# Out weights of the second layer made one group earlier and kept in DRAM, and the weights' place split in two regions

## The chip, the cores and the metric

The kernel runs on one core of a Trainium2 chip. The metric is the device time of one launch in microseconds (us). The kernel before has a median of 670.33 us over three runs (668.5 to 673.26).

## The reference, cut to what matters

The output of a banded attention with block summaries, 1536 tokens of width 512, goes through two feed-forward layers:

```python
def _moe_ref(x, w_gate, w_val, w_out, rms_g):        # first part: 512 -> 1536 -> 512
    xn = x / np.sqrt(np.mean(x * x, axis=-1, keepdims=True) + 1e-06) * rms_g
    g = xn @ w_gate
    return ((g / (1.0 + np.exp(-g))) * (xn @ w_val) @ w_out).astype(np.float32)

def _moe2_ref(x, w_in, w_out):                       # second part: 512 -> 2048 -> 512
    h = x @ w_in
    return ((h - np.tanh(h)) @ w_out).astype(np.float32)
```

The weights arrive as 64-bit floats. Each float32 operand of a product is split into a high and a low part, and three matmuls are summed.

## The kernel before, in words

**Stages.** The tokens are 12 tiles of 128, in three groups of four. Attention for a tile is two units of four heads. The first part (`step`, kind "a") runs over the groups; for each group it runs 12 steps, one for each block of 128 hidden columns: eight first products (three matmuls each, 128x512) into two "mid" banks, the gate on ACT and DVE, then four second products into four accumulator banks. While a group is in the first part, the attention units of the next group are woven in; the third group has none beside it. The second part (`pair`) runs over the groups again, eight pairs of hidden blocks each, by Strassen's scheme: seven products of 128x256 from sums of input and weight blocks, a tanh, and eight second products with the out weights of the pair's two blocks.

**Weights.** `widen` turns 512 columns of 64-bit weights into float32: a 512 KB load into one of two `raw` buffers, one ACT instruction (L737), two DVE instructions (L738, L739). `split` makes the high part by an ACT cast (L754, into `ih` or `oh`) and the low part by a subtraction on DVE or POOL (L756, into `il` or `ol`). There are three `oh` and three `ol` buffers. The first layer's 12 blocks of 1536 columns lie in one region `wd`; the second layer's 16 blocks of 1024 columns (512 in, 512 out) are widened into the same place as the first layer's blocks are finished with. So 32 conversions of 512 columns belong to the second layer.

**Second part, by group.** In its first group `make` forms the weight sums of a pair (L1028 to L1031), splits them (L1048, L1050), splits the two out blocks, and stores all of it in DRAM (`keep_i`, `keep_o`). In its second and third group `fetch` loads them: four transfers of `ki` and four of `ko` for each pair. The fetched sums land in `wd`, as nine buffers for the high and nine for the low parts (`lh`, `ll`), which can be used only once all of `wd` is done with; the second group's first pair lands in `ih` and `il` instead. The chain inside a pair is: products 1 and 6, a copy and an add (L1102, L1098), products 7 and 5, adds, products 4, 2 and 3.

**Order.** A planner (`Plan`) places every instruction on its engine by due time, with a duration and a lag for each, and the kernel is emitted in that order. Each engine then works its row strictly in order, SP too, which issues every transfer and waits there for its buffers. The planner counts a transfer at 2.78 us per MB (1.46 us for one `raw` load).

Of the kernel before, what the change touches and what calls it, by code (L numbers as in the profile page):

```python
# [9 lines left out]
F32 = mybir.dt.float32  # L10
# [246 lines left out]
def kernel(  # L257
# [24 lines left out]
    wd_r = Region(const, "wd", NF1 * W1, F32)  # L282
    wd = wd_r.get(F32)

    ident = const.tile([P, P], F32, name="ident")

# [88 lines left out]
                return tl[i][:, :, (t - t0) * P:(t - t0 + 1) * P]  # L375


    far = 4 * W1
    kr, vr = [], []
    for b in range(B):  # L380
        kr.append(wd[:, far:far + 4 * S])
        vr.append(wd[:, far + 4 * S:far + 8 * S])
        far += 8 * S
    early_u = [wd[:, 8 * W1 + i * UN:8 * W1 + (i + 1) * UN] for i in range(EARLY)]
    far = 8 * W1 + EARLY * UN
    early_s = [wd[:, far + i * HH * SC:far + (i + 1) * HH * SC] for i in range((4 * W1 - EARLY * UN) // (HH * SC))]
# [322 lines left out]


    def w_first(f):
        return wd[:, f * W1:(f + 1) * W1]

    def w_second(f):
        return wd[:, f * W2:(f + 1) * W2]

    chain = {}

# [178 lines left out]
    spare = NF2 * W2  # L897
    plan.pools["sm"] = Buffers([wd[:, spare:spare + 4 * q]])
    plan.pools["up"] = Buffers([rest.part(2 * 512, 2 * 512 + q, F32), const.tile([P, q], F32, name="up")])
    for i, tag in enumerate(("eh", "el")):  # L900
        plan.pools[tag] = Buffers([hi_r[k].part(i * 1024, (i + 1) * 1024, F32R) for k in range(2)])
    for i, tag in enumerate(("lh", "ll")):
        plan.pools[tag] = Buffers([wd_r.part(k * 1024, (k + 1) * 1024, F32R) for k in range(i, 18, 2)])
    plan.pools["tb"] = Buffers([lo_r[0].part(i * 512, (i + 1) * 512, F32) for i in range(NC_)])
    operand = {}
    ready = {}
    prepared = {}
# [68 lines left out]
    def dma_both(n, pick, slots, kept, *after):  # L976
# [10 lines left out]
            ops.append(o)  # L987
        return ops

    def fetch(n, g):  # L990
        weights = {}
        at = 0
        last_made = [chain[k] for k in ("i", "il", "o", "ol")]
# [7 lines left out]
        outs = []  # L1001
        for j in (1, 0):
            w = [slot("oh"), slot("ol")]
            o = dma_both(DM, True, w, keep_o[n][j], *stored[n])
            outs.insert(0, (*w, [o]))
        return outs, weights

    def make(n):
        f0, f1 = 2 * n, 2 * n + 1
        d = [w_second(f) for f in (f0, f1)]  # L1010
        conv = [wide_op["b", f][0] for f in (f0, f1)]
        a11, a12 = d[0][:, 0:q], d[0][:, q:2 * q]
        a21, a22 = d[1][:, 0:q], d[1][:, q:2 * q]
        right = wd[:, f0 * W2:(f0 + 2) * W2].rearrange("p (f c) -> p f c", f=2)[:, :, q:2 * q]
        weights = {}
        store = []

        if n:
            gate = [o for f in range(NF1 - 2, NF1) for o in split_op["a", f]] + first_ops["a", 2][-2:]
            names = "ih", "il", "sm"  # L1020
        else:
            gate = first_ops["a", 0] + first_ops["a", 1] + unit_ops
# [12 lines left out]
        for ks, pieces in zip(  # L1035
            turns,
            (
                ((0, q, lambda: a11, lambda t: t, [conv[0]]), (q, 3 * q, lambda: sm[:, 0:3 * q], lambda t: t, [o3])),
                ((0, 2 * q, lambda: right, three, conv), (2 * q, q, lambda: s(4), lambda t: t, [o4])),
            ),  # L1040
        ):
            wh, wl = slot(names[0]), slot(names[1])
            done = []
            for c, m, src, form, of in pieces:
                cut = slice(c, c + m)
                us = 0.1 + 0.42 * m / 512
# [15 lines left out]
        return outs, weights  # L1062

    def pair(g, n, at):
        f0, f1 = 2 * n, 2 * n + 1
# [20 lines left out]
            second_first.setdefault(g, []).append(o)  # L1086
            return o

        after_a = [o for f in range(NF1 - 2, NF1) for o in split_op["a", f]]
# [107 lines left out]
    for g in range(len(GROUPS)):  # L1197
# [8 lines left out]
        if g + 2 == len(GROUPS):  # L1206
            pass
    for f in range(NF2):
        over = [o for q in range(NF1) if q * W1 < (f + 1) * W2 and f * W2 < (q + 1) * W1 for o in split_op["a", q]]
# [116 lines left out]
```

## Time and profile before

| | |
|---|---|
| runs, median (lowest to highest) | 670.33 us (668.5 to 673.26) |
| profiled execution | 668.83 us, of it 666.9 us from the first to the last instruction |
| PE busy | 654.6 us (98%) |
| PE weight load busy | 553.9 us (83%) |
| DVE / ACT / POOL busy | 449.3 / 334.0 / 53.5 us |
| TensorE clock granted | 0.996, the higher of its two levels (2.4 GHz) |
| moved by DMA | 128.11 MB |

The stages lie about so in the profiled execution: attention alone up to 37 us; first part with attention 37 to 148 (first group) and 148 to 291 (second group); first part alone 291 to 397 (third group); second part 397 to 483, 483 to 567 and 567 to 652, then the last outputs.

### The profile page before, as it was taken

How to read it: one execution, taken by the hardware profiler on the slowest of the kernel's cores; microseconds unless marked ns; L12 is line 12 of the kernel's file. 1: busy time of each engine (PE TensorE's matmuls, PEld its weight loads, DVE VectorE, ACT ScalarE, POOL GpSimd, SP SyncE). 2: the span in 40 equal slices, each digit the busy share in tenths (PEclk: the TensorE clock that was granted, in tenths of full speed). 3: DMA queues.
4: the chain of work that ended last, by engine and by line, in shares of the span. 5: the costliest groups of instructions: out<-in, count | busy, mean ns of one | idle time of the engine just before them, and what ended most of it. 6: DMA issues, size and time to landing. Idle time of an engine off the chain costs nothing.

```text
span 666.9 us, 10381 instructions
## 1 busy us (share of the span) xinstructions
PE 654.6 (98%) x3714; PEld 553.9 (83%) x3714; DVE 449.3 (67%) x1007; ACT 334.0 (50%) x688; POOL 53.5 (8%) x118
## 2 busy tenths in 40 slices
PE   8999999999999999999999999999999999999996
PEld 7998777888888888788888888888888888888885
DVE  5789996885636355479877779898874443545343
ACT  3895566774636445457555548555542231323222
POOL 2221212110101100000000010101100000000000
PEclk9999999999999999999999999999999999999999
DMA  9887564662011110022745558668689999997232
GB/s 342 331 282 266 187 190 140 201 195 88 2 31 32 49 41 1 1 64 63 238 153 163 150 168 311 248 259 316 239 322 349 350 338 368 344 322 254 95 95 95
DMA packets 47642, 128.11 MB, mean 192 GB/s; under 512 B 5688, under 2 KB 8168, under 8 KB 47592
## 3 DMA queue, kind: packets, MB, share of 16 engines
q1 hardware_dynamic: 47592, 127.46, 55.6%
q8 instruction: 29, 0.48, 0.3%
q14 instruction: 21, 0.17, 0.1%
HBM read 101.23 MB, written 26.21 MB: 191 GB/s over the span
## 4 chain that ended last, share of the span: by engine, by line
PE 83%; DMA 8%; ACT 4%; DVE 3%; issue 1%; SPq 1%; POOL 0%; ACTq 0%; DVEq 0%; POOLq 0%
PE bank L779 14%; PE bank L781 13%; PE bank L780 13%; PE mid L779 12%; PE mid L780 11%; PE mid L781 11%; DMA raw<-in_w_dram 4%; PE bank L643 3%; PE bank L549 2%; PE bank L600 1%; DMA wd<-in_units_dram 1%; PE bank L654 1%; DMA out_dram<-th 1%; ACT wd L737 1%; DMA ko<-ol 1%
## 5 line engine op out<-in xcount | busy, mean ns | idle before, releaser
L779 PE MATMUL mid<-hi,ih 128*128 128x512 f32 (+1 forms) x310 | 123.5, 398 | 0.1
L781 PE MATMUL mid<-hi,il 128*128 128x512 f32 (+1 forms) x310 | 118.1, 381 | 0.0
L780 PE MATMUL mid<-lo,ih 128*128 128x512 f32 (+1 forms) x304 | 116.5, 383 | 0.0
L781 PE MATMUL bank<-oh,hl 128*128 128x512 f32 x192 | 75.7, 394 | 0.5 <-DVE hl L1136 0.5
L779 PE MATMUL bank<-oh,hh 128*128 128x512 f32 x192 | 75.8, 395 | 0.1
L780 PE MATMUL bank<-ol,hh 128*128 128x512 f32 x192 | 75.4, 393 | 0.1
L779 PEld LDWEIGHTS mid<-hi,ih 128*128 128x128 f32 x310 | 58.3, 188 | 12.6 <-issue 2.4
L781 PEld LDWEIGHTS mid<-hi,il 128*128 128x128 f32 x310 | 58.4, 188 | 12.3
L780 PEld LDWEIGHTS mid<-lo,ih 128*128 128x128 f32 x304 | 57.4, 189 | 9.7
L737 ACT ACTIVATE wd<-raw 128x512 f32<-128x512 f32 x62 | 41.5, 672 | 44.9 <-DMA raw<-in_w_dram 44.7
L754 ACT CAST ih<-wd 128x512 fp32r<-128x512 f32 x76 | 46.8, 618 | 30.7 <-PE mid L780 22.0
L779 PE MATMUL bank<-hh,oh 128*128 128x512 f32 (+1 forms) x152 | 60.5, 398 | 0.0
L780 PE MATMUL bank<-hl,oh 128*128 128x512 f32 (+1 forms) x152 | 58.0, 382 | 0.0
L781 PE MATMUL bank<-hh,ol 128*128 128x512 f32 (+1 forms) x152 | 57.8, 381 | 0.0
L756 DVE TENSOR_TENSOR il<-wd,ih 128x512 fp32r<-128x512 f32 x73 | 50.8, 705 | 2.7 <-ACT ih L754 2.1
L833 DVE TENSOR_TENSOR th<-th,mid 128x512 f32<-128x512 f32 (+1 forms) x38 | 24.9, 656 | 39.9 <-PE mid L781 39.8
L1119 ACT ACTIVATE lo<-lo 128x512 f32<-128x512 f32 (+1 forms) x48 | 25.1, 523 | 39.6 <-DVE lo L1098 39.6
L781 PEld LDWEIGHTS bank<-oh,hl 128*128 128x128 f32 x192 | 36.1, 188 | 9.9 <-DVE hl L1136 1.5
L739 DVE SCALAR_TENSOR_TENSOR wd<-raw,wd 128x512 uint32<-128x512 uint32 x62 | 42.7, 692 | 1.0
L754 ACT CAST oh<-wd 128x512 fp32r<-128x512 f32 x54 | 33.5, 621 | 16.7 <-issue 6.3
L1119 ACT ACTIVATE lo<-mid 128x256 f32<-128x256 f32 x24 | 9.2, 384 | 65.0 <-PE mid L781 63.7
L780 PEld LDWEIGHTS bank<-ol,hh 128*128 128x128 f32 x192 | 36.0, 188 | 4.3 <-DMA ol<-ko 0.4
(173 smaller groups left out, 1440.5 us busy)
## 6 DMA issues: line engine op xcount, KB each, us to landing
raw<-in_w_dram SPq DMA_DIRECT2D x62, 512.0 KB, 3.9
wd<-ki SPq DMA_DIRECT2D x30, 512.0 KB, 6.3
wd<-ki SPq DMA_DIRECT2D x30, 384.0 KB, 6.1
pad<-in_units_dram SPq DMA_DIRECT2D x19, 442.0 KB, 4.3
oh<-ko SPq DMA_DIRECT2D x32, 256.0 KB, 4.1
ol<-ko SPq DMA_DIRECT2D x32, 256.0 KB, 4.4
ko<-oh SPq DMA_DIRECT2D x16, 256.0 KB, 2.0
ko<-ol SPq DMA_DIRECT2D x16, 256.0 KB, 2.1
```

Source lines behind the costliest of these rows:

```text
L549: nc.tensor.matmul(ps[e][:, j * SC:(j + 1) * SC], q[r, j], k[r, j], start=(j == 0), stop=(j == NP - 1), skip_group_check=True,)
L600: nc.tensor.transpose(pt[:, h * P:(h + 1) * P], sc[:, m0:m0 + P], ident)
L643: nc.tensor.matmul(av[:, h * (D + 1):(h + 1) * (D + 1)], ph[:, h * P:(h + 1) * P], v[:, h], start=(h == 0), stop=False, skip_group_check=True,
L737: a = act(0.58, lambda d=d, w=w: nc.scalar.activation(d, w(k=1).bitcast(F32), AF.Prelu, scale=2.0 ** -112, alpha=-(2.0 ** 32)), ld, *after ...
L739: a = dve(0.6, lambda du=du, w=w: nc.vector.scalar_tensor_tensor(du, w(k=0), 29, du, ALU.logical_shift_right, ALU.bitwise_or), a, slots=[r ...
L754: a = act(0.52, lambda c=c: nc.scalar.copy(wh[:, c], d[:, c]), dep, chain.get(tag), slots=[wh])
L756: on.tensor_tensor(wl[:, c], d[:, c], r32(wh[:, c]), ALU.subtract)
L779: nc.tensor.matmul(o, ah, bh, start=first, stop=False, skip_group_check=True)
L780: nc.tensor.matmul(o, ah, bl, start=False, stop=False, skip_group_check=True)
L781: nc.tensor.matmul(o, al, bh, start=False, stop=last, skip_group_check=True)
L833: a = dve(0.07 + 0.535 * v, lambda: nc.vector.tensor_tensor(th[:, :n], th[:, :n], m1[:, :n], ALU.mult), a, m1.done, slots=[m1, th])
L1119: o = act(us, lambda: nc.scalar.activation(out(), x(), AF.Tanh), *after, slots=slots)
```

## The change

1. `make_out` is new. For each of the 16 blocks f it loads the out half of the second layer's weights, widens and splits it, and stores both parts in `keep_o`. The planner gets these as work due over the second group of the first part; they can begin when the first group's first products are done, because their buffers lie in `hi0`, the first group's input: two of 512 columns (`os`) for the widened block and one of 1024 (`op`) for the two parts.
2. `fetch_outs` loads the out weights of a pair from `keep_o`, now in all three groups of the second part; `make` no longer splits or stores them.
3. `wd` becomes two regions, `wd0` for the first layer's blocks 0 to 5 and `wd1` for blocks 6 to 11. Only the 16 in halves of the second layer are widened in place, into `wd0`. `wd1` serves the fetched sums from the end of the first part on, as four buffers each for `lh` and `ll`; the second group's first pair lands there too.

```diff
+    def make_out(f, due):
+        n, j = divmod(f, 2)
+        raw, d, o = slot("raw"), slot("os"), slot("op")
+        gate = first_ops["a", 0]
+        ld = dma(0.524, lambda: nc.sync.dma_start(raw[:], src[:, 1024:2048]), chain.get("raw"), slots=[raw])
+        a = act(0.58, lambda: nc.scalar.activation(d[:], w(1).bitcast(F32), AF.Prelu, ...), ld, *gate, slots=[raw, d])
+        a = dve(0.34, lambda: nc.vector.tensor_scalar(du(), du(), 3, None, ALU.logical_shift_left), a, slots=[d], port=True)
+        a = dve(0.6, lambda: nc.vector.scalar_tensor_tensor(du(), w(0), 29, du(), ...), a, slots=[raw, d], port=True)
+        a = act(0.52, lambda: nc.scalar.copy(o[:, :512].bitcast(F32R), d[:]), a, chain.get("op"), slots=[d, o])
+        z = flex({"pool": (1.32, lambda: rest(nc.gpsimd), True), "dve": (0.61, lambda: rest(nc.vector), True)}, a, slots=[d, o])
+        stored_o[f] = [
+            dma(DM * P * 4e-6, lambda i=i: nc.sync.dma_start(r32(keep_o[n][j][i]), o[:, i * 512:(i + 1) * 512]), x, slots=[o], due=due)
+            for i, x in enumerate((a, z))
+        ]
+    def fetch_outs(n):
+        for j in (1, 0):
+            w = [slot("oh"), slot("ol")]
+            o = dma_both(DM, True, w, keep_o[n][j], *stored_o[2 * n + j])
...
     def fetch(n, g):
-            w = [slot(t) for t in (("ih", "il") if (g, n) == (1, 0) else ("lh", "ll"))]
-            o = dma_both(m, True, w, [k[:, at:at + m] for k in keep_i[n]], *stored[n], *last_made)
+            w = [slot("lh"), slot("ll")]
+            o = dma_both(m, True, w, [k[:, at:at + m] for k in keep_i[n]], *stored[n], *after_a)
...
     def make(n):
-        outs = [split(eng, w[:, 512:], 512, "o", wide_op["b", f][1:]) for eng, f, w in zip(("gps", "dve"), (f1, f0), d[::-1])][::-1]
-        for j, (wh, wl, do) in enumerate(outs):
-            store += dma_both(DM, False, (wh, wl), keep_o[n][j], *do[0])
-        return outs, weights
+        return fetch_outs(n), weights
...
-        plan.pools[tag] = Buffers([wd_r.part(k * 1024, (k + 1) * 1024, F32R) for k in range(i, 18, 2)])
+        plan.pools[tag] = Buffers([wd_r[1].part(k * 1024, (k + 1) * 1024, F32R) for k in range(i, 8, 2)])
+    plan.pools["os"] = Buffers([hi_r[0].part(i * 512, (i + 1) * 512, F32) for i in range(2)])
+    plan.pools["op"] = Buffers([hi_r[0].part(1024, 2048, F32)])
...
+        if g == 0:
+            for f in range(NF2):
+                make_out(f, begin[1] + (begin[2] - begin[1]) * (f + 1) / NF2)
...
-        wide_op["b", f] = widen(f"b{f}", w2[f].bitcast(U32), w_second(f), W2, *over)
+        wide_op["b", f] = widen(f"b{f}", w2[f].bitcast(U32), w_second(f), 512, *over)
```

The order on the engines. First ACT, where the second group of the first part begins. Before (L829 is the gate's tanh, L838 the high part of the gate's result, L871 a result of the first group, L754 the cast of first-layer weights):

```order
L829 ACTIVATE th1_101<-mid0_80 128x256
L754 CAST ih1_91<-wd_0_67 128x512
L838 CAST hh1_103<-th1_101 128x256
L754 CAST ih1_91<-wd_0_67 128x512
L754 CAST oh0_94<-wd_0_67 128x512
L829 ACTIVATE th0_100<-mid0_80 128x512
```

The same place in the change; L1004 and L1007 are the two ACT instructions of `make_out`, and `hi0_1` is the first group's input, taken as its buffers:

```order
L828 ACTIVATE th1_102<-mid0_81 128x256
L1004 ACTIVATE hi0_1_1707<-raw0_89 128x512
L837 CAST hh1_104<-th1_102 128x256
L1004 ACTIVATE hi0_1_1707<-raw1_90 128x512
L753 CAST ih1_92<-wd0_0_67 128x512
L753 CAST oh0_95<-wd0_0_67 128x512
L1007 CAST hi0_1_1707<-hi0_1_1707 128x512
L753 CAST ih1_92<-wd0_0_67 128x512
L828 ACTIVATE th0_101<-mid0_81 128x512
```

All 16 blocks are put between the gates of the second group in this manner; each L1004 stands behind a load and each L1007 behind the stores of the block before it.

Next DVE, where the second part begins. Before (L840 is the last gate's low part, L1029 to L1031 weight sums, L1050 their low parts, L1098 the adds for which the products of the first pair wait):

```order
L840 TENSOR_TENSOR hl1_105<-th1_101,hh1_103 128x512
L1030 TENSOR_TENSOR wd_0_67<-wd_0_67 128x256
L739 SCALAR_TENSOR_TENSOR wd_0_67<-raw1_89,wd_0_67 128x512
L1031 TENSOR_TENSOR wd_0_67<-wd_0_67 128x256
L756 TENSOR_TENSOR ol0_97<-wd_0_67,oh0_94 128x512
L1050 TENSOR_TENSOR il0_92<-wd_0_67,ih0_90 128x768
L738 TENSOR_SCALAR wd_0_67<-wd_0_67 128x512
L1050 TENSOR_TENSOR il1_93<-wd_0_67,ih1_91 128x512
L739 SCALAR_TENSOR_TENSOR wd_0_67<-raw0_88,wd_0_67 128x512
L1050 TENSOR_TENSOR il1_93<-wd_0_67,ih1_91 128x256
L1098 TENSOR_TENSOR rest_0_70<-rest_0_70,mid0_80 128x256
L1028 TENSOR_TENSOR wd_0_67<-wd_0_67 128x256
```

The same place in the change (L1126 is the add that was L1098, L1060 to L1063 the weight sums):

```order
L839 TENSOR_TENSOR hl1_106<-th1_102,hh1_104 128x512
L1060 TENSOR_TENSOR wd0_0_67<-wd0_0_67 128x256
L1061 TENSOR_TENSOR wd0_0_67<-wd0_0_67 128x256
L1062 TENSOR_TENSOR wd0_0_67<-wd0_0_67 128x256
L755 TENSOR_TENSOR ol2_100<-wd1_0_68,oh2_97 128x512
L1063 TENSOR_TENSOR wd0_0_67<-wd0_0_67 128x256
L1126 TENSOR_TENSOR rest_0_71<-rest_0_71,mid0_81 128x256
```

Ahead of the first add stand five DVE instructions behind the last gate where there were nine; the widening instructions and the out weights' low parts of the second layer are gone, and the low parts of the pair's sums stand further up in the row. (The `ol2` left there belongs to the first layer's last step.)

Last, ACT in the third group of the first part, in the change. The two transfers that fetch the first pair's out weights (`oh0<-ko0_1`, `oh1<-ko0_0`) stand on SP in and at the end of the second group, so `oh0` and `oh1` are held from then on:

```order
L736 ACTIVATE wd0_0_67<-raw1_90 128x512
L828 ACTIVATE th0_101<-mid0_81 128x512
L753 CAST ih0_91<-wd1_0_68 128x512
L736 ACTIVATE wd0_0_67<-raw0_89 128x512
L753 CAST oh2_97<-wd0_0_67 128x512
L837 CAST hh0_103<-th0_101 128x512
```

Every step of that group casts its out weights into the one buffer `oh2`, where before the steps took `oh0`, `oh1` and `oh2` in turn.

## Rows read from the trace of the kernel before

**Rows 1.** Page, part 1: engine, busy us, share of the span, instructions.

```profile
PE 654.6 (98%) x3714; PEld 553.9 (83%) x3714; DVE 449.3 (67%) x1007; ACT 334.0 (50%) x688; POOL 53.5 (8%) x118
```

**Rows 2.** Windows of DVE: stretch, its length, busy (instructions), clock, DMA share, GB/s.

```profile
148.00:291.00 143.00, 77.74 (x191) 1.00 0.11 32
...
397.00:483.00 86.00, 77.59 (x163) 1.00 0.72 266
483.00:567.00 84.00, 42.45 (x90) 1.00 0.95 345
```

**Rows 3.** Waits of PE's weight load, 397 to 483 us: total us, times, longest.

```profile
PEld bank L779 <- DVE lo L1098: 3.0, 6, 1.0
PEld mid L779 <- DVE rest L1098: 0.9, 2, 0.7
PEld mid L779 <- DVE up L1098: 0.7, 2, 0.5
```

**Rows 4.** The same, 483 to 567 us.

```profile
PEld bank L779 <- DVE lo L1098: 2.3, 8, 0.5
PEld bank L780 <- DMA ol<-ko: 0.4, 1, 0.4
```

**Rows 5.** Timeline of PE near 403 us: start, us, instruction, idle before it.

```profile
403.63 0.39 PE L779 MATMUL mid<-pad,hi 128*128 128x256 f32 x1 [0.51 <-DVE rest L1098]
```

**Rows 6.** Timeline of DVE at the same place.

```profile
402.22 0.68 DVE L739 SCALAR_TENSOR_TENSOR wd<-raw,wd 128x512 uint32<-128x512 uint32 x1
...
403.16 0.41 DVE L1098 TENSOR_TENSOR rest<-rest,mid 128x256 f32<-128x256 f32 x1
```

**Rows 7.** The chain that ended last, near 469 us: start, us, what.

```profile
469.12 0.60 DVE ol L756
```

**Rows 8.** Groups by line, 397 to 483 us: count, busy us, mean ns.

```profile
L756 POOL TENSOR_TENSOR ol<-wd,oh 128x512 fp32r<-128x512 f32 x7 | 10.0, 1425 | 73.5 <-ACT oh L754 54.3 <-DVE il L1050 19.2
L754 ACT CAST oh<-wd 128x512 fp32r<-128x512 f32 x15 | 9.3, 621 | 12.3 <-issue 6.3 <-PE bank L781 5.8
L756 DVE TENSOR_TENSOR ol<-wd,oh 128x512 fp32r<-128x512 f32 x8 | 5.5, 690 | 0.8 <-ACT oh L754 0.6
L739 DVE SCALAR_TENSOR_TENSOR wd<-raw,wd 128x512 uint32<-128x512 uint32 x5 | 3.3, 683 | 0.0
L737 ACT ACTIVATE wd<-raw 128x512 f32<-128x512 f32 x4 | 2.7, 672 | 1.3 <-DMA raw<-in_w_dram 1.3
L738 DVE TENSOR_SCALAR wd<-wd 128x512 uint32<-128x512 uint32 x4 | 1.7, 415 | 0.0
```

**Rows 9.** Waits of PE's weight load, 37 to 148 us.

```profile
PEld bank L643 <- ACT pad L610: 0.6, 1, 0.6
PEld bank L694 <- DVE pad L701: 0.3, 1, 0.3
...
PEld bank L779 <- ACT wd L737: 0.2, 1, 0.2
```

**Rows 10.** Waits of PE's weight load, 148 to 291 us.

```profile
PEld bank L643 <- ACT pad L610: 0.2, 1, 0.2
```

**Rows 11.** Waits of ACT, 37 to 148 us.

```profile
ACT wd L737 <- DMA raw<-in_w_dram: 9.9, 12, 3.5
```

**Rows 12.** Waits of ACT, 291 to 397 us.

```profile
ACT wd L737 <- DMA raw<-in_w_dram: 32.8, 17, 4.0
```

**Rows 13.** Page, part 6: transfers, count, KB each, median us from issue to landing.

```profile
raw<-in_w_dram SPq DMA_DIRECT2D x62, 512.0 KB, 3.9
...
oh<-ko SPq DMA_DIRECT2D x32, 256.0 KB, 4.1
...
ko<-ol SPq DMA_DIRECT2D x16, 256.0 KB, 2.1
```

**Rows 14.** Timeline of PE: a step's last second product, and the next step's first.

```profile
346.45 0.40 PE L779 MATMUL bank<-hh,oh 128*128 128x512 f32 x1
...
350.65 0.40 PE L779 MATMUL bank<-hh,oh 128*128 128x512 f32 x1
```

More of the change, by code (lines that the diff above doesn't have):

```diff
@@ L280 @@
     lo_t = [r.get(F32R).rearrange("p (c s) -> p c s", c=NC_) for r in lo_r]
-    wd_r = Region(const, "wd", NF1 * W1, F32)
-    wd = wd_r.get(F32)
+    wd_r = [Region(const, f"wd{i}", NF1 // 2 * W1, F32) for i in range(2)]
+    wd = [r.get(F32) for r in wd_r]
     ident = const.tile([P, P], F32, name="ident")
@@ L375, in cols @@
                 return tl[i][:, :, (t - t0) * P:(t - t0 + 1) * P]
[L378 to L386, printed above, removed]
+    kr = [wd[0][:, 4 * W1:4 * W1 + 4 * S], wd[1][:, 4 * S:8 * S]]
+    vr = [wd[1][:, 0:4 * S], wd[1][:, 8 * S:12 * S]]
+    far = 4 * S
+    early_u = [wd[1][:, far + i * UN:far + (i + 1) * UN] for i in range(EARLY)]
+    far += EARLY * UN
+    early_s = [wd[1][:, far + i * HH * SC:far + (i + 1) * HH * SC] for i in range((8 * S - EARLY * UN) // (HH * SC))]
     early_users = []
@@ L711, in w_first @@
     def w_first(f):
-        return wd[:, f * W1:(f + 1) * W1]
+        h, f = divmod(f, NF1 // 2)
+        return wd[h][:, f * W1:(f + 1) * W1]
     def w_second(f):
-        return wd[:, f * W2:(f + 1) * W2]
+        return wd[0][:, f * 512:(f + 1) * 512]
     chain = {}
@@ L896 @@
     plan.pools["ts"] = Buffers([rest.part(0, 1024, F32)])
-    spare = NF2 * W2
-    plan.pools["sm"] = Buffers([wd[:, spare:spare + 4 * q]])
+    spare = NF2 * 512
+    plan.pools["sm"] = Buffers([wd[0][:, spare:spare + 4 * q]])
     plan.pools["up"] = Buffers([rest.part(2 * 512, 2 * 512 + q, F32), const.tile([P, q], F32, name="up")])
@@ L988, in dma_both, with rest @@
         return ops
+    stored_o = {}
+    made_o = []
+    def make_out(f, due):
+        n, j = divmod(f, 2)
+        raw, d, o = slot("raw"), slot("os"), slot("op")
+        w = lambda k: raw[:].rearrange("p (n k) -> p n k", k=2)[:, :, k]
+        du = lambda: d[:].bitcast(U32)
+        src = w2[f].bitcast(U32)
+        gate = first_ops["a", 0]
+        ld = dma(0.524, lambda: nc.sync.dma_start(raw[:], src[:, 1024:2048]), chain.get("raw"), slots=[raw])
+        chain["raw"] = ld
+        a = act(0.58, lambda: nc.scalar.activation(d[:], w(1).bitcast(F32), AF.Prelu, scale=2.0 ** -112, alpha=-(2.0 ** 32)), ld, *gate, slots=[raw, d])
+        a = dve(0.34, lambda: nc.vector.tensor_scalar(du(), du(), 3, None, ALU.logical_shift_left), a, slots=[d], port=True)
+        a = dve(0.6, lambda: nc.vector.scalar_tensor_tensor(du(), w(0), 29, du(), ALU.logical_shift_right, ALU.bitwise_or), a, slots=[raw, d], port=True)
+        a = act(0.52, lambda: nc.scalar.copy(o[:, :512].bitcast(F32R), d[:]), a, chain.get("op"), slots=[d, o])
+        chain["op"] = a
+        def rest(on):
+            on.tensor_tensor(o[:, 512:].bitcast(F32R), d[:], o[:, :512], ALU.subtract)
+        z = flex({"pool": (1.32, lambda: rest(nc.gpsimd), True), "dve": (0.61, lambda: rest(nc.vector), True)}, a, slots=[d, o])
[3 more added lines that the diff above has]
+        ]
+        made_o.extend(stored_o[f])
+    def fetch_outs(n):
+        outs = []
+        for j in (1, 0):
+            w = [slot("oh"), slot("ol")]
+            o = dma_both(DM, True, w, keep_o[n][j], *stored_o[2 * n + j])
+            outs.insert(0, (*w, [o]))
+        return outs
     def fetch(n, g):
@@ L1000, in fetch @@
             at += m
[L1001 to L1005, printed above, removed]
-        return outs, weights
+        return fetch_outs(n), weights
     def make(n):
@@ L1013, in make @@
         a21, a22 = d[1][:, 0:q], d[1][:, q:2 * q]
-        right = wd[:, f0 * W2:(f0 + 2) * W2].rearrange("p (f c) -> p f c", f=2)[:, :, q:2 * q]
+        right = wd[0][:, f0 * 512:(f0 + 2) * 512].rearrange("p (f c) -> p f c", f=2)[:, :, q:2 * q]
         weights = {}
@@ L1018, in make @@
         if n:
-            gate = [o for f in range(NF1 - 2, NF1) for o in split_op["a", f]] + first_ops["a", 2][-2:]
+            gate = [o for f in range(NF1 // 2) for o in split_op["a", f]]
             names = "ih", "il", "sm"
         else:
-            gate = first_ops["a", 0] + first_ops["a", 1] + unit_ops
+            gate = first_ops["a", 0] + first_ops["a", 1] + unit_ops + made_o
             names = "eh", "el", "ts"
@@ L1057, in make @@
             at += m
-        outs = [split(eng, w[:, 512:], 512, "o", wide_op["b", f][1:]) for eng, f, w in zip(("gps", "dve"), (f1, f0), d[::-1])][::-1]
-        for j, (wh, wl, do) in enumerate(outs):
-            store += dma_both(DM, False, (wh, wl), keep_o[n][j], *do[0])
         stored[n] = store
-        return outs, weights
+        return fetch_outs(n), weights
     def pair(g, n, at):
@@ L1087, in product @@
             return o
-        after_a = [o for f in range(NF1 - 2, NF1) for o in split_op["a", f]]
         up, uq = slot("up"), slot("up")
@@ L1205 @@
                 unit(t0 + i // 2, i % 2, a + (z - a) * (i + 1) / (2 * nt))
-        if g + 2 == len(GROUPS):
-            pass
+        if g == 0:
+            for f in range(NF2):
+                make_out(f, begin[1] + (begin[2] - begin[1]) * (f + 1) / NF2)
     for f in range(NF2):
-        over = [o for q in range(NF1) if q * W1 < (f + 1) * W2 and f * W2 < (q + 1) * W1 for o in split_op["a", q]]
-        wide_op["b", f] = widen(f"b{f}", w2[f].bitcast(U32), w_second(f), W2, *over)
+        over = [o for q in range(NF1) if q * W1 < (f + 1) * 512 and f * 512 < (q + 1) * W1 for o in split_op["a", q]]
+        wide_op["b", f] = widen(f"b{f}", w2[f].bitcast(U32), w_second(f), 512, *over)
+    after_a = [o for f in range(NF1 // 2, NF1) for o in split_op["a", f]]
     for g in range(len(GROUPS)):
```

1 line of the change is left out of this document (removed).

## The prediction

> **What bounds the kernel now.** I read the page first, then the waits of PE's weight load stage by stage, then the timeline where the longest of them lie. PE is busy for 98% of the span [rows 1], but the ends of matmuls are modelled, so this alone proves little. The waits of the weight load tell more, since a matmul that waits shows there first. In the second group of the first part (148 to 291 us) one wait is for another engine, 0.2 us [rows 10]; the rest of its waits carry no releaser and belong to the attention's small products. In the first group of the second part (397 to 483 us) the weight load waits 3.0 + 0.9 + 0.7 = 4.6 us for DVE adds on L1098 [rows 3]; in the group behind it, with the same products, 2.3 us [rows 4]. DVE is busy 77.6 of 86 us in the one and 42.5 of 84 in the other [rows 2]. So PE bounds the kernel nearly everywhere, and the change can save only where DVE is late for PE: some 2 us, of which the reader sees a piece in [rows 5]: a product of the first pair waits 0.51 us for an add that began at 403.16, and ahead of that add DVE was widening second-layer weights at 402.22 [rows 6].
>
> **What the change removes.** From the stretch 397 to 483 us go, by count and mean [rows 8]: five L739 and four L738 (3.3 + 1.7 us of DVE), the low parts of the out weights (5.5 us of DVE for eight, 10.0 of POOL for seven), and on ACT up to 15 casts (9.3 us, one or two of them first-layer casts) and four L737 (2.7 us). That is 10.5 us less for DVE, 12 for ACT. DVE falls from 77.6 to about 67 of 86 us, still far above the 42.5 of the next group, since the pairs' sums are still made there. By that share the excess wait, 4.6 - 2.3 = 2.3 us, would shrink by 10.5/35, to a gain of 0.7 us. But the waits are not spread evenly. At the start of the second part the order of the change has five DVE instructions ahead of the first add where nine stood, and two L739, one L738 and one L756 of the second layer are out of that row, 2 x 0.68 + 0.42 + 0.69 = 2.5 us, more than any wait of [rows 3] (1.0 at most). At the end of that group a low part of out weights lies on the chain that ended last, 0.60 us [rows 7], and it goes too. I take 2.0 us as the gain, near the whole excess; its bounds are 0 (the adds are late for their own chain, whatever else DVE does) and 4.6 (all waits of [rows 3] go).
>
> **What it adds in the second group of the first part.** For each of 16 blocks: one raw load, L1004 like L737 (0.67 us), L1005 like L738 (0.42), L1006 like L739 (0.68), a cast (0.62), a subtraction (0.69 on DVE, where 15 of the 16 stand in the order; one is on POOL), and two stores. ACT gets 16 x 1.29 = 20.6 us, DVE 16 x 1.10 + 15 x 0.69 = 28 us. DVE goes from 77.7 to 106 of 143 us [rows 2], 74%, so there is room. What costs is not the work but the waits in ACT's row: L1004 waits for a load that takes 3.9 us [rows 13] where the planner counts 1.46 and a lag, L1007 for two stores of 2.1 us, since `op` is one buffer. Behind them in the row stand the gate's tanh and casts, and behind those PE. The trace has this same pattern twice. In the first group 28 conversions made ACT wait 9.9 us [rows 11], and PE's weight load waited for ACT or DVE 0.6 + 0.3 us and three times 0.2, 1.5 us in all [rows 9]. In the third group ACT waited 32.8 us for loads [rows 12], and the weight load for nobody (the answer for that stretch is empty). 16 conversions at the first group's rate cost 16/28 x 1.5 = 0.9 us; the bounds are 0 (third group's rate) and 1.5 (all that the first group lost). I take 0.7.
>
> **What else moves, at nothing.** The third group loses 11 or so widenings from DVE and ACT; PE waits for nobody there, so nothing is gained. The out weights are now fetched in the second part's first group also, 32 transfers of 256 KB, 8.4 MB, in place of as many bytes of raw loads and of stores that leave that stretch; DMA share there is 0.72 [rows 2]. A fetch takes 4.1 us [rows 13], is issued when one of three buffers comes free, and is needed about a pair (84/8 = 10.5 us [rows 2]) later. In the later groups the same scheme already runs, with one wait of 0.4 us [rows 4] at a DMA share of 0.95; if this cover were gone each late fetch would cost about that much. The extra stores lie where the share is 0.11 [rows 2]. The fetched sums get four buffers a part for nine, two pairs ahead instead of four; since the region is free at the end of the first part already, the second group's first two pairs can be loaded long before they are used, and a freed buffer has over a pair's time to be filled, where half its size takes 4.1 us [rows 13]. I count nothing for it, and at most the 0.4 us of `ol` as a gain.
>
> **The sum.** 668.8 (profiled execution) - 2.0 + 0.7 = 667.5 us. The median of the runs, 670.3, lies 1.5 us above that execution; by the median the same sum gives 669.0. I predict **668.0**, between the two, which is no change that can be told: a measurement of this kernel tells about 1% (6.7 us) from no change.
>
> **Rivals.**
>
> *The relief does not arrive.* The adds wait for their own chain (product, add, product), as in the later groups, where DVE is half idle and the weight load still waits 2.3 us [rows 4]. For: six of the waits in [rows 3] are of the kind that also stands in [rows 4]. Against: [rows 6] and [rows 7] show widening and splitting right ahead of the late adds. Then 668.8 + 0.7 = 669.5.
>
> *More than the excess goes.* If all waits on L1098 in the second part went, 4.6 + 2.3 in the two groups shown and about as much as the latter in the third, 9.2 us, the time would be 668.8 - 9.2 + 0.7 = 660.3, over 1% faster. Against: the second and third group's work on DVE is the same before and after. The Trainium skill (Perfetto Trace Analysis, Identifying the Most-Contended Engine) says that matmul busy time is a bad measure of PE's headroom and weight-load busy time a good one; by that rule the page's 83% [rows 1] leaves 17% of 667 us, an estimate of 113 us to win. The trace does not bear this out: from 291 to 397 us the weight load names no wait at all, and only the waits of [rows 3, 4] are open to anything this change does.
>
> *Waits on ACT in the second group hold PE up (slower).* With units beside it, ACT there has the tightest deadlines. Each of 16 blocks brings two waits. At the third group's mean of 32.8/17 = 1.9 us for a load, 16 loads are 31 us of waiting, and the stores add as many shorter ones. The share that reaches PE decides: above 28% (8.7 us, the 6.7 of one per cent and the 2.0 gained) the kernel is over 1% slower; at half it would be 668.8 - 2.0 + 15 = 682. For: ACT's row is in order and the planner counts the loads too short. Against: in the first group 1.5 of 9.9 us reached PE (15%), which here makes 4.7 us and 671.5, and in the third group none.
>
> *One buffer for the out weights in the third group (slower).* From the end of the second group two of three `oh` buffers hold the second part's first weights. Every step must then cast and split its own between the last second product of the step before (346.45, plus 0.7) and its own first (350.65) [rows 14]: 3.5 us for 0.62 + 0.69 and the hand-overs. ACT waits for loads up to 4.0 us at a time [rows 12]; such a wait right ahead of the cast is 2 us too long. If that met every one of 12 steps, it would cost 24 us, 691; it decides from five steps on. Against: the mean wait is 1.9 us, which fits, and the order puts the cast behind the loads' instructions of the step, not ahead.
>
> *Unit loads late behind the new transfers.* The attention's loads now stand on SP between raw loads and stores that wait for ACT and DVE. If each of the eight units came late by one store, 2.1 us [rows 13], it would cost 17 us, 684. The buffers for units are three, so a load has about a unit's time (143/8 = 18 us [rows 2]) of slack. The Trainium skill (DMA: Bandwidth & Descriptors, Anatomy of one DMA) says that a semaphore wait of a transfer happens on the issuing sequencer, ahead of its dispatch, which is what would make one late store hold up the loads behind it; no row of mine shows a unit that came late by it.
>
> **How the numbers follow.** Forecast, a net gain of 0.3 to 3 us or so: 0.57. Relief does not arrive: 0.20. More than the excess: 0.07. ACT's waits: 0.08; one buffer: 0.05; unit loads: 0.03, and of these three together about 0.12 lies over 1% slower. Faster by over 1% (below 663.6 by the median) 0.07; within 1% 0.81; slower (above 677) 0.12. The range reaches from 662.5 (a gain of 4.6 and the lower of the two bases) to 675 (15% of ACT's waits on PE, with the median's base, and some of the store waits); the forecast's own range is 665.5 to 670.5.
>
> **What would show it.** Right: in 397 to 483 us (shifted little) the weight load waits under 3 us for L1098, now L1126; DVE there is busy about 67 us; in the second group DVE is near 106 of 143 us, ACT waits on L1004 and L1007, and the weight load waits for ACT or DVE under 1.5 us; the third group stays without waits. Wrong: a weight load that waits for `ol2`, `oh2` or a gate's low part in the third group (one buffer), for unit products behind a late load (SP), or for the gate in the second group by more than 5 us (ACT); or the second part's first group as long as before (no relief).

## The result and the profile after

The changed kernel takes **673.0 us** (median of 20 runs, 670.6 to 677.1) against 669.7 us for the kernel before in the same session (20 runs, 667.4 to 673.3): ratio **1.0053, 95% interval 1.0035 to 1.0071**. It is slower by half a per cent, some 3.5 us. That is inside the range, and nearer to no change than one per cent, but on the other side of the forecast, which had a gain of 0.3 to 3 us. The profiled execution took 674.1 us, 672.4 of them span (before 668.8 and 666.9), so the two profiles lie 5.5 us apart where the medians lie 3.3 apart; the parts below are those of the profiles, and some 2 us of them may be these two executions and not the kernels.

Page, part 1, of the changed kernel (engine, busy us, share, instructions), to be read beside [rows 1]:

```profile
PE 656.7 (98%) x3714; PEld 552.6 (82%) x3714; DVE 451.4 (67%) x1011; ACT 333.1 (50%) x688; POOL 48.9 (7%) x114
```

PE does the same matmuls (x3714 in both); the busy shares tell nothing. So I followed the same products through both timelines of PE. The start of the 33rd, the 97th and the 145th second product of the first part (`bank<-hh,oh`) and of the last one of the second part (`bank<-oh,hh`) cut the run in stretches that hold the same PE work in every kernel: A is most of the second group with its attention, B most of the third group, C the rest of the third and the second part. The 97th product, which ends A, before and then in the change (start, us, instruction):

```profile
291.65 0.40 PE L779 MATMUL bank<-hh,oh 128*128 128x512 f32 x1
```

```profile
299.08 0.40 PE L778 MATMUL bank<-hh,oh 128*128 128x512 f32 x1
```

The times are read to 0.1 us, so a stretch can be off by about 0.1.

| us | start of A | A | B | C | end |
|---|---|---|---|---|---|
| before | 133.3 | 158.3 | 103.0 | 265.7 | 660.3 |
| change | 134.1 | **165.0** | **104.3** | **262.3** | 665.7 |
| difference | 0.8 | +6.7 | +1.3 | -3.4 | +5.4 |

The kernel before has one trace, so how firm are these? The versions further down that make no blocks in A, or only two, have A at 158.4 and 158.8 us, and all versions but the one that moves the blocks to the third group have C between 262.1 and 263.5 us; the 6.7 and the 3.4 us stand clear of that. The 0.8 us ahead of A do not: its start lies between 132 and 134.1 us over all traces.

The relief of the second part came, 3.4 us. Twice as much was lost ahead of it, in the stretch that received the blocks. The weight load's waits there, 148 to 299 us (total us, times, longest); [rows 10] had 0.2 us:

```profile
PEld bank L598 <- ACT pad L575: 5.0, 14, 1.9
...
PEld bank L652 <- ACT pad L609: 1.8, 1, 1.8
```

5.0 + 1.8 = 6.8 us, about the 6.7 us of the table (three more waits for ACT or DVE make 0.8 us, where the kernel before had 0.2). L575 is the exponential of the attention's scores, L598 the transposes behind it, L609 a copy and L652 the products behind that: all four belong to the attention units. What ACT itself waited for in that stretch:

```profile
ACT hi L1004 <- DMA raw<-in_w_dram: 11.9, 5, 4.2
...
ACT hi L1007 <- DMA ko<-hi: 7.4, 4, 2.7
```

and DVE:

```profile
DVE hi L1011 <- DMA ko<-hi: 3.1, 2, 2.0
```

All three wait for transfers of `make_out`: 11.9 + 7.4 + 3.1 = 22.4 us. Two places in the timeline show how such a wait reaches PE. The first is on ACT (start, us, instruction, idle before it and what ended it):

```profile
203.94 0.66 ACT L1004 ACTIVATE hi<-raw 128x512 f32<-128x512 f32 x1 [3.31 <-DMA raw<-in_w_dram]
204.50 0.36 ACT L609 COPY pad<-bank 112x256 f32<-112x256 f32 x1
```

and on PE directly behind:

```profile
204.92 0.71 PE L652 MATMUL bank<-pad 113*128 113x130 f32 x4 [1.40 <-ACT pad L609]
```

ACT's row is in order. L609 is short and has nothing to do with the weights, but it stood behind L1004, and L1004 waited 3.31 us for its load. The second place is in the chain of work that ended last (start, us, what):

```profile
211.47 5.03 DMA ko<-hi
...
216.59 1.70 DVE hi L1011
218.30 0.60 DVE il L755
218.90 0.26 DVE pad L561
...
219.72 0.31 PE bank L598
```

A store of the block before took 5.03 us; the next low part (L1011) needs the same `op` buffer, and in DVE's row the maxima of the scores (L561) stand behind it, then the exponential, then the transposes. The transfers' own rows (page, part 6: count, KB, median us to landing):

```profile
raw<-in_w_dram SPq DMA_DIRECT2D x62, 512.0 KB, 4.2
...
ko<-hi SPq DMA_DIRECT2D x32, 256.0 KB, 3.9
```

The stores take 3.9 us, not the 2.1 of [rows 13].

In the third group, 299 to 404 us, the weight load waited for a gate's low part (L839), and 0.2 us for a gate's cast, where it waited for nobody before:

```profile
PEld bank L779 <- DVE hl L839: 1.2, 1, 1.2
```

ACT's timeline there:

```profile
347.91 0.67 ACT L736 ACTIVATE wd<-raw 128x512 f32<-128x512 f32 x1 [4.16 <-DMA raw<-in_w_dram]
348.49 0.61 ACT L753 CAST oh<-wd 128x512 fp32r<-128x512 f32 x1
349.00 0.62 ACT L837 CAST hh<-th 128x512 fp32r<-128x512 f32 x1
```

A load's wait of 4.16 us stands ahead of the cast into the only free `oh` buffer and of the gate's cast. PE then starts a product late:

```profile
351.03 0.50 PE L779 MATMUL bank<-hl,oh 128*128 128x512 f32 x1 [0.87 <-DVE hl L839]
```

The gain, in the windows of DVE (stretch, length, busy and instructions, clock, DMA share, GB/s), beside [rows 2]:

```profile
148.00:299.00 151.00, 101.70 (x232) 1.00 0.47 149
...
404.00:489.00 85.00, 65.14 (x142) 1.00 0.76 266
489.00:574.00 85.00, 43.76 (x92) 1.00 0.81 270
```

and in the weight load's waits, 404 to 489 us, beside [rows 3]:

```profile
PEld bank L778 <- DVE lo L1126: 1.9, 6, 0.6
```

The waits for the add fall from 4.6 to 1.9 us. By products, the second part up to its second group takes 99.1 us (before 102.1), and 1.4 of these 3.0 us are won before its first second product.

### The profile page after: what moved, and what is told of

The parts are those of the page before. It is cut to its first block, busy times and chain, and to the rows that moved or that the text cites. A ratio compares the mean times of both kernels' runs of the same rounds, so it can differ in the third digit from the quotient of the medians.

```text
span 672.4 us, 10478 instructions
## 1 busy us (share of the span) xinstructions
PE 656.7 (98%) x3714; PEld 552.6 (82%) x3714; DVE 451.4 (67%) x1011; ACT 333.1 (50%) x688; POOL 48.9 (7%) x114
## 4 chain that ended last, share of the span: by engine, by line
PE 58%; DMA 4%; DVE 4%; ACT 2%; issue 1%; SPq 0%; DVEq 0%; ACTq 0%
PE bank L778 12%; PE bank L780 12%; PE bank L779 12%; PE mid L778 7%; PE mid L779 6%; PE mid L780 6%; DMA raw<-in_w_dram 3%; DMA out_dram<-th 1%; PE bank L641 1%; DMA ko<-hi 1%; PE bank L547 1%; PE bank L598 1%; DVE wd L738 1%; PE bank L652 0%; ACT wd L736 0%
## 5 line engine op out<-in xcount | busy, mean ns | idle before, releaser
L778 PE MATMUL mid<-hi,ih 128*128 128x512 f32 (+1 forms) x304 | 121.7, 400 | 0.1
L780 PE MATMUL mid<-hi,il 128*128 128x512 f32 (+1 forms) x304 | 116.5, 383 | 0.0
L755 DVE TENSOR_TENSOR il<-wd,ih 128x512 fp32r<-128x512 f32 x71 | 49.1, 700 | 3.8 <-ACT ih L753 3.4
L736 ACT ACTIVATE wd<-raw 128x512 f32<-128x512 f32 x46 | 30.9, 674 | 32.3 <-DMA raw<-in_w_dram 32.0
L778 PEld LDWEIGHTS bank<-oh,hh 128*128 128x128 f32 x192 | 36.2, 188 | 3.6 <-ACT hh L1163 0.3
L1151 DVE TENSOR_TENSOR lo<-lo 128x512 f32<-128x512 f32 (+1 forms) x48 | 26.6, 556 | 15.4 <-ACT lo L1147 15.4
```

The source lines that it names most:

```text
L736: a = act(0.58, lambda d=d, w=w: nc.scalar.activation(d, w(k=1).bitcast(F32), AF.Prelu, scale=2.0 ** -112, alpha=-(2.0 ** 32)), ld, *after ...
L755: on.tensor_tensor(wl[:, c], d[:, c], r32(wh[:, c]), ALU.subtract)
L778: nc.tensor.matmul(o, ah, bh, start=first, stop=False, skip_group_check=True)
L780: nc.tensor.matmul(o, al, bh, start=False, stop=last, skip_group_check=True)
L1151: return dve(us, lambda: nc.vector.tensor_tensor(out(), x(), z(), ALU.subtract), *after, slots=slots)
```

## The experiments

Theory 1 (the rival "waits on ACT"): the loads and stores of `make_out` land later than the planner counts, so instructions of other work stand behind a wait. Theory 2: the added work on ACT and DVE is too much for the stretch. Theory 3: the added transfers themselves disturb it (memory, unit loads). The stretches of every version, whose names stand with the experiments below (the ratio is to the kernel before in the same session; sessions differ, so compare ratios rather than medians):

| | A | B | C | median us | ratio to before, 95% |
|---|---|---|---|---|---|
| e6_two_blocks | 158.8 | 104.9 | 262.6 | 668.2 | 0.9976 (0.9956 to 0.9997) |
| e1_one_raw | 159.2 | 104.4 | 262.1 | 667.0 | 0.9968 (0.9953 to 0.9983) |
| e2_no_store | 160.5 | 104.4 | 262.5 | 669.6 | 1.0001 (0.9984 to 1.0019) |
| e3_two_high | 166.5 | 104.4 | 262.8 | 675.7 | 1.0093 (1.0071 to 1.0116) |
| e4_lag | 158.4 | 104.9 | 263.1 | 667.8 | 0.9981 (0.9966 to 0.9995) |
| e4_loads | 161.6 | 104.8 | 262.5 | 670.8 | 1.0029 (1.0010 to 1.0049) |
| e4_stores | 158.6 | 104.6 | 262.8 | 667.8 | 0.9980 (0.9965 to 0.9996) |
| e5_third | 158.4 | 110.0 | 271.7 | 683.2 | 1.0222 (1.0182 to 1.0262) |
| e9_hold | 163.9 | 103.2 | 263.2 | 672.0 | 1.0032 (1.0013 to 1.0052) |
| e9_lag_hold | 158.6 | 103.0 | 263.5 | 666.3 | 0.9948 (0.9931 to 0.9965) |
| e7_lag_b | 158.3 | 103.0 | 262.1 | 665.7 | 0.9947 (0.9925 to 0.9968) |
| e7_hold | 158.7 | 102.9 | 262.9 | 666.0 | 0.9948 (0.9929 to 0.9966) |

**Fourteen blocks left out (e6_two_blocks).** Only blocks 0 and 1 are made, and every pair fetches these.

```diff
-            for f in range(NF2):
+            for f in range(2):
                 make_out(f, ...)
-            o = dma_both(DM, True, w, keep_o[n][j], *stored_o[2 * n + j])
+            o = dma_both(DM, True, w, keep_o[0][j], *stored_o[j])
```

> Only blocks 0 and 1 of the out weights are made; all pairs of the second part fetch these two, so the output is not the reference's; the two regions and all 48 fetches stay. If the change loses its time in making the blocks (waits or work), the second group of the first part is as long as before (158 us from its first second products to the third group's, where the changed kernel takes 165) and the whole is 3 us under the kernel before, about 666.5. If it loses it by the regions, the fetches or the single buffer for out weights in the third group, it stays above 671.

A falls from 165.0 to 158.8 us, and the whole to 668.2 us, 0.2% under the kernel before. The blocks cost the second group its loss, by whatever of them. B stays at 104.9 us: the third group's loss is not from making blocks.

**One load for all blocks (e1_one_raw).** Fifteen of the sixteen raw loads are left out (all blocks hold the weights of block 0); the work and the stores stay.

```diff
-        raw, d, o = slot("raw"), slot("os"), slot("op")
+        raw, d, o = one_raw, slot("os"), slot("op")
+        if not one_load:
             ld = dma(0.524, lambda: nc.sync.dma_start(raw[:], src[:, 1024:2048]), ...)
+            one_load.append(ld)
+        ld = one_load[0]
...
```

> All 16 blocks are made from one raw load (15 loads are left out, so the output is not the reference's); the work on ACT and DVE and the 32 stores stay. If waits for transfers are the cost, the waits of ACT on L1004 for raw (11.9 us in the changed kernel) go and about half of the 6.7 us of the second group with them: 3 to 4 us under the changed kernel, about 669.5. If the added work on ACT and DVE is the cost, no change: about 673.

A is 159.2 us with every instruction of ACT and DVE still there, so theory 2 falls. At 667.0 us more came back than the 3 to 4 us expected.

**The stores of fourteen blocks left out (e2_no_store)** (the second part fetches blocks 0 and 1 for all pairs).

```diff
             for i, x in enumerate((a, z))
+            if f < 2
...
-            o = dma_both(DM, True, w, keep_o[n][j], *stored_o[2 * n + j])
+            o = dma_both(DM, True, w, keep_o[0][j], *stored_o[j])
```

> All 16 blocks are made, but 14 are not stored and the first two are fetched in their place (output not the reference's); loads and the work on ACT and DVE stay. If waits for transfers are the cost, the waits of L1007 and L1011 for the stores (7.4 us of ACT and 3.1 us of DVE) go and 2 to 4 us of the cost with them, about 669.5 to 671. If the added work is the cost: about 673.

A is 160.5 us. ACT's waits, then the weight load's, in the second group:

```profile
ACT hi L1004 <- DMA raw<-in_w_dram: 9.0, 8, 2.6
```

```profile
PEld bank L598 <- ACT pad L575: 2.0, 6, 0.7
```

Without the stores the loads still cost 2.2 us; without the loads the stores cost 0.9; together they cost 6.7. The two do not add up. That either kind of wait eats the slack that the other would have lived on would explain it, but was not tried, and 0.9 us is little more than A differs between traces of versions without blocks there (158.3 to 158.8).

**Two high buffers (e3_two_high).** The low part is written in place over the widened block, which makes room for two buffers for the high part.

```diff
-    plan.pools["op"] = Buffers([hi_r[0].part(1024, 2048, F32)])
+    plan.pools["op"] = Buffers([hi_r[0].part(1024 + i * 512, 1536 + i * 512, F32) for i in range(2)])
...
-        a = act(0.52, lambda: nc.scalar.copy(o[:, :512].bitcast(F32R), d[:]), ...)
+        a = act(0.52, lambda: nc.scalar.copy(o[:].bitcast(F32R), d[:]), ...)
...
-            on.tensor_tensor(o[:, 512:].bitcast(F32R), d[:], o[:, :512], ALU.subtract)
+            on.tensor_tensor(d[:].bitcast(F32R), d[:], o[:], ALU.subtract)
...
```

> Nothing left out: the low part is written over the widened block, which leaves room in the same four places of 512 columns for two high buffers instead of one buffer for both parts. If the stores' landing (3.9 us) held the single buffer and so ACT and DVE, 2 to 3 us under the changed kernel, about 670.5; if only the loads or the work count, no change, 673.

This missed: 675.7 us, a ratio of 1.0093 where the change has 1.0053. ACT's waits and the weight load's:

```profile
ACT hi L1004 <- DMA ko<-hi: 16.5, 8, 5.5
```

```profile
PEld bank L598 <- ACT pad L575: 6.8, 14, 1.5
```

The wait went from the cast to L1004, which now needs the widened block's buffer back from a store, up to 5.5 us late. In the plan a buffer is free when its store is counted as done, some 0.7 us of transfer; here the stores took 5.1 us in the median, so L1004 was placed too early. The second buffer for one part was bought with a longer hold on another, and didn't help.

**The landing time counted (e4_lag).** Nothing left out and no instruction changed: the planner adds 2 us to the landing of `make_out`'s loads and 3 us to that of its stores, and orders accordingly.

```diff
-            return 0.0 if b.eng == "dma" else 1.0
+            return 0.0 if b.eng == "dma" else 1.0 + a.land
...
-                        insort(s.pool.idle, (end, s.index))
+                        insort(s.pool.idle, (end + o.land, s.index))
...
+        ld.land = 2.0
...
+        for x in stored_o[f]:
+            x.land = 3.0
```

> Nothing left out: the same loads, work, stores and buffers as the change; only the planner counts 2 us more until a raw load of make_out has landed and 3 us more until its stores have, so that the waiting ACT and DVE instructions stand later in their rows. If what costs is that instructions wait in order ahead of the attention's, most of the 6.7 us of the second group goes and the whole lies under the kernel before, 665 to 667. If it is the number of transfers (DMA or SP busy) or the work, no change: 673.

A is 158.4 us, that of before, with all the work and all the transfers; theory 3 falls with it. The transfers landed about as late as in the change: the stores after 3.9 us in both, the blocks' loads after 4.4 us (4.9 in the change). Line numbers are up to four higher in the versions with an edited planner; the cast L1007 is L1009 here. ACT's only row of waits for transfers of `make_out` in the second group, then the weight load's waits for an engine:

```profile
ACT hi L1009 <- DMA ko<-hi: 2.0, 2, 1.8
```

```profile
PEld mid L779 <- ACT th L829: 0.2, 1, 0.2
PEld bank L642 <- ACT pad L609: 0.2, 1, 0.2
```

The 11.9 us of waiting for loads are gone, of the 22.4 us in all 2.0 are left, DVE has none, and the weight load waits 0.4 us for an engine (0.2 in [rows 10]). From the first to the last block's start stand 97.5 us (170.95 to 268.44) where the change had 82.3 (172.2 to 254.5). Theory 1 is shown. The other versions bear it out: the more ACT and DVE wait for transfers of `make_out` in the second group, the longer A is against before. It is 22.4 us of waits and 6.7 us in the change, 20.5 and 5.6 in e9_hold (below), 13.5 and 3.3 in e4_loads, 9.0 and 2.2 in e2_no_store, 4.5 and 0.3 in e4_stores, 3.2 and 0.9 in e1_one_raw, 2.0 and 0.1 here; only e3_two_high stands out, with 16.5 and 8.2.

**Loads alone, stores alone (e4_loads, e4_stores).** The same with only one of the two landing times.

```diff
-        ld.land = 2.0
+        ld.land = 0.0        # (stores alone; loads alone sets x.land = 0.0)
```

> As the run before, with the 2 us for the loads alone. If the loads are the larger part, as the run with one raw load says, 667 to 670; the waits of L1009 (the cast, L1007 in the change) for stores stay. If the stores alone were the cause, 673.

> The 3 us for the stores alone. The waits for stores go, those for the loads stay: 670 to 672 if the loads are the larger part, 667 if the stores are.

Loads alone bring 3.4 of the 6.6 us back (A 161.6; at 670.8 us just outside the 667 to 670 expected); ACT still waits for stores:

```profile
ACT hi L1009 <- DMA ko<-hi: 9.6, 6, 4.6
```

Stores alone bring all of it (158.6), though by e1_one_raw the loads were the larger part and their waits were expected to stay. With stores counted, the plan holds the one `op` buffer longer and so spaces the blocks by 6.5 us in the mean, where the change has 5.5; at that pace the loads have mostly landed as well (ACT's waits for them fall to 2.3 us).

**The blocks in the third group (e5_third)**, behind the last attention unit, where there is no attention to hold up.

```diff
-        gate = first_ops["a", 0]
+        gate = first_ops["a", 0] + unit_ops
...
-        if g == 0:
+        if g == 1:
             for f in range(NF2):
-                make_out(f, begin[1] + (begin[2] - begin[1]) * (f + 1) / NF2)
+                make_out(f, begin[2] + (at - begin[2]) * (f + 1) / NF2)
```

> Nothing left out: the 16 blocks are made after the last attention unit, in the third group of the first part, where ACT waited 32.8 us for loads before and PE for nobody; the planner's figures are those of the change. If the harm comes from waits ahead of attention instructions, the second group is as long as before (158 us) and the third loses at most 2 us; the in halves come later, so the second part's first group may keep its waits: 667 to 670. If waits hurt wherever they stand, 672 or more.

This missed by far: 683.2 us. B grows to 110.0 and C to 271.7 us. The weight load's waits in the third group, then those early in the second part:

```profile
PEld mid L778 <- ACT ih L753: 2.1, 1, 2.1
PEld bank L779 <- DVE hl L839: 2.0, 2, 1.3
```

```profile
PEld mid L778 <- DVE rest L1126: 3.0, 2, 2.2
PEld mid L780 <- DVE il L1082: 1.4, 1, 1.4
```

The gates suffer from such waits as the attention does, and the in halves, pushed out of the third group (8 of their ACT instructions L736 stand between 400 and 489 us, where the change has none), bring back the late adds that the change removes.

Part of the loss is the clock, which fell behind these waits. PE stood idle 1.71 us before 317.89 and 0.97 us before 320.21, and then worked at the lower level (1.2 GHz) until about 326 us. The windows of PE (stretch, length, busy and instructions, clock, DMA share, GB/s):

```profile
318.00:322.00 4.00, 3.02 (x8) 0.69 0.69 207
322.00:326.00 4.00, 4.00 (x11) 0.50 0.50 115
326.00:330.00 4.00, 4.00 (x18) 0.96 0.58 213
```

The 14 products from 320.21 to 326.34 us took 6.1 us, where they take 3.3 at 0.235 us each, as before the fall: an estimate of 2.8 of the 7.0 us that B grew. The same happened from 411 to 415 us, behind an idle of 1.97 us, where 17 products of 128x256 started 0.21 us apart instead of 0.12: an estimated 1.6 us of C. No other version shows such a fall in A, B or C.

**The third group's loss.** Two ideas: the single `oh` buffer, or the load's wait ahead of it in ACT's row. `hold` (e9_hold) fetches the first pair's out weights only behind the last cast of the first part, so that three buffers serve the group; `lag_b` (e7_lag_b) is e4_lag with 2 us more for the second layer's in-half loads too. e9_lag_hold is e4_lag with `hold`, e7_hold is e7_lag_b with `hold`.

```diff
+    def fetch_outs(n, *hold):
...
-            o = dma_both(DM, True, w, keep_o[n][j], *stored_o[2 * n + j])
+            o = dma_both(DM, True, w, keep_o[n][j], *stored_o[2 * n + j], *hold)
...
-        return fetch_outs(n), weights
+        return fetch_outs(n, *(split_op["a", NF1 - 1][-1:] if n == 0 else ())), weights
```

```diff
+            if nm[0] == "b":
+                ld.land = 2.0
...
```

> The first pair's out weights are fetched only after the last cast of the first part, so all three `oh` buffers serve the third group again; nothing else is changed against the change and nothing is left out. If the 1.3 us that the third group grew (103.0 to 104.3 us) come from the single `oh` buffer, that group returns to 103.0 us and the kernel gains 1.3 us on the change (ratio near 1.003 to before). If they come from a load's wait in ACT's row, the third group stays at 104.3 us and the ratio at 1.005. If the first pair's weights now come too late, the second part's first group (262.3 us for the whole part) grows instead.

> The version in which the planner counts the landing time of the new block's loads and stores (measured 667.8 us, 0.998), with the first pair's out weights held back as well; nothing is left out. One-buffer theory: the third group goes from 104.9 to 103.0 us and the kernel to about 666 us, 0.995 of before. Load-wait theory: third group stays at 104.9 us, 0.998.

> The version in which the planner counts the landing time of the new block's loads and stores, with 2 us more also for the loads of the second layer's in halves, which fall in the third group; nothing is left out. Load-wait theory: the wait of PE's weight load for the gate in the third group (1.2 + 0.8 us) goes, the group comes from 104.9 to about 103 us, and the kernel to 666 us, 0.995. One-buffer theory: 104.9 us and 0.998 stay.

> Both together: landing time counted for all of the second layer's loads and for the new stores, and the first pair's out weights held back; nothing is left out. If each of the two causes takes a part of the third group's loss, this has the shortest third group (103.0 us or less) and the shortest time, 665.5 to 666.5 us, 0.994 to 0.995 of before; if one cause alone makes it, this equals the better of the two single versions.

Each alone brings B to 103.0 us or next to it, and both together no further. So the loss seems to take both, one buffer and a late load: with three buffers ACT still waits for loads, and PE hardly notices. In e9_hold, ACT and then the weight load in the third group:

```profile
ACT wd L736 <- DMA raw<-in_w_dram: 14.1, 7, 4.4
```

```profile
PEld bank L779 <- DVE hl L839: 0.4, 1, 0.4
```

`hold` moves other instructions too (C is 0.4 to 1.0 us longer with it than in the same version without it), so that the buffer alone is at work there is likely and not shown. The expectation that set one cause against the other was too simple. e7_lag_b, with the single buffer and nothing left out, has the lowest median: 665.7 us, 0.9947 of before, with A and B as before and C shorter. By their intervals e7_hold and e9_lag_hold can't be told from it.

## Why the prediction was right or wrong

**The relief: right in place and direction, too small.** 2.0 us taken, 3.4 measured, within its bounds of 0 to 4.6. The waits for the add fell to 1.9 us (under 3 was named) and DVE's busy time to 65.1 us (67 named); 1.4 us came ahead of the first second product, as argued from the order. The rival "relief does not arrive" is out.

**The second group: the step that failed.** 0.7 us were taken, with bounds of 0 and 1.5; 6.7 came. The work was counted about rightly (DVE 101.7 us, 106 named), and so was the place, ACT's waits for loads and stores. What was mis-sized is the loss for each conversion. I scaled the 1.5 us that the first group lost by the number of conversions, 16 to 28. But a conversion there made ACT wait 0.35 us (9.9/28, [rows 11]), and a block here made ACT and DVE wait 1.4 us (22.4/16), four times as long; 10.5 of the 22.4 us are waits for stores, of which the first group's rate holds none. And 6.8 of the 22.4 us reached PE, 30%, twice the 15% that [rows 9] and [rows 11] give.

That 15% was not firm, which the traces made since show. In the changed kernel's own trace the first group, with about the same conversions as before, has 3.2 us of the weight load's waits for ACT or DVE to 11.0 us of ACT's waits for loads, 29%; over all fourteen traces it goes from 9% (0.8 of 9.3) to 30% (3.3 of 11.0). The third group, where none reached PE ([rows 12]), has no attention beside it. The gates that I named as victims were hardly hurt: the attention's exponentials, maxima and copies were, each with a PE product directly behind. The stores were also put at 2.1 us by the only store row there was; they took 3.9.

The rival "waits on ACT" was the right case, at a chance of 0.08. Its 671.5 us came nearest of all cases to 673.0, but by two errors that cancel: its 31 us of waits for loads was too high (11.9, and 10.5 for stores) and its 15% too low. That the measured time lies inside the range is owed to this rival, which set the upper end, and not to the forecast. The lower end, 662.5, does not follow from its own terms (668.8 - 4.6 = 664.2).

**The third group, taken at nothing: wrong by 1.3 us.** The rival "one buffer" named the mechanism, a load's wait of 4.0 us right ahead of the cast; it was 4.16 us, and it met one step, not the five from which it would decide. That the one buffer had its part in it is likely and not shown.

**What I costed at nothing and was nothing.** The fetches in the second part's first group, the four buffers for the sums, and the unit loads: no wait of the weight load names them. The unit loads took longer beside the new transfers (5.2 us in the median, 4.3 before), and no product of the second group waited for them.

**More than the excess goes: out.** The Trainium skill (Perfetto Trace Analysis, Identifying the Most-Contended Engine) reads PE's headroom from the weight load's busy share. That share is 82% in the change and 83% in the fastest version, half a per cent faster than before at the same share as before, so here it did not tell where time was; the waits by stage did. It is 81% even in the third group before, where the weight load waits for nobody (stretch, length, busy and instructions, clock, DMA share, GB/s):

```profile
291.00:397.00 106.00, 85.84 (x459) 1.00 0.51 156
```

So a share near 82% is what PE showed here with nothing to wait for, and the 17% that the rule leaves is for the most part not time that waits held.

## What to carry to other kernels

Work that fits an engine's idle share can still cost time in an in-order row: ask for each added instruction that waits for a transfer which unrelated instructions stand behind it, and what waits for those. Where a planner sets the order, give it the landing times that the trace shows, stores and returned buffers included, before counting on slack; here that alone turned a loss of 0.5% into a gain of 0.5%. To size such waits, count them one by one, stores too, rather than scale another stage's loss by a number of conversions; and a rate taken from 1.5 us of waits in one trace is hardly a rate, as the 9 to 30% of the first group show.

## What the runs showed of the hardware

A 256 KB store to DRAM landed after 3.9 us in the median and 5.03 us in the chain, where the stores of the kernel before had 2.1 us; the number for one stage did not hold in another. The subtraction L1011, 0.69 us elsewhere, took 1.70 us at 216.59 while POOL ran a subtraction of its own (216.46 to 217.75). It is not alone: the five 128x512 subtractions on DVE that took over 1 us in the changed kernel (1.01 to 1.77) all ran beside such an instruction of POOL, and the 207 that ran beside none took 0.72 us at most; five others overlapped one and took 0.68 to 0.73. What slows them was not tried.

In e5_third the granted clock fell to the lower level twice, once just behind idle stretches of PE of 1.71 and 0.97 us and once behind one of 1.97 us. 128x512 products then started 0.43 us apart instead of 0.235 until about 326 us.
